# Gated linear attention, then a multiplicative FFN: keeping x in SBUF and starting the FFN's gates earlier

## The chip, the cores and the metric

The kernel runs on one core of a Trainium2 chip. The time is the device time of one execution in microseconds (us), the median of several runs. Engines are named as in the profile: PE is TensorE (PEld its weight load), DVE is VectorE, ACT is ScalarE, POOL is GpSimd, and SP is SyncE, which issues nearly all DMAs here.

## The reference, cut to what matters

```python
B, H, S, D = 4, 8, 768, 48                    # q, k, v, alpha
n_tokens, d_model, d_ff = 3072, 384, 1024     # w1, w2: [384, 1024]; w3: [1024, 1024]; w_out: [1024, 384], in float64

for t in range(S):
    state = alpha[:, :, t, :, None] * state + einsum('bhd,bhe->bhde', k[:, :, t], v[:, :, t])
    y[:, :, t] = einsum('bhd,bhde->bhe', q[:, :, t], state)
x = y.transpose(0, 2, 1, 3).reshape(B * S, H * D)
a = x @ w1
b = x @ w2
h = a * b @ w3
return (h @ w_out).astype(float32)
```

The recurrence is linear in the state. The kernel works it off in chunks of 128 time steps: inside a chunk by scores and a mask, between chunks by a state of 48 x 48 per head. There are 4 x 6 = 24 chunks. Three chunks of x, 384 tokens, form a group; the FFN's gates (x @ w1 times x @ w2) work on one of the 8 groups and 128 of the 1024 columns at a time, so there are 64 gate tiles. w3 is folded into w_out once (8 folds), and the output is 24 blocks of 128 tokens. The weights w1, w2, w3, w_out arrive as float64 and are converted on chip from their bit patterns.

## The kernel before

x of one chunk is left by TensorE in two PSUM banks: bank i holds heads of parity i, with 64 partitions per head (48 of them used), two heads one above the other, and two such pairs (j) along the free dimension. ScalarE copies the banks to SBUF, and two DMAs per chunk write them to DRAM in an order in which the 384 rows are head by head, 48 rows each. A group is loaded back as 3 blocks of 128 rows.

```python
ps = pool("ps", 8, space=PSUM)
xp = pool("xp", 1)
work = pool("work", 2, ...)
xd = [dram.tile([DM, TG], FP32, name=f"xd{g}") for g in range(NG)]        # DM = 384, TG = 384

def to_fp32(dst, *srcs):                       # float64 to float32, in steps
    n, m = len(srcs) * srcs[0].shape[1], srcs[0].shape[1]
    raw = rawp.tile([C, n], I64, tag="raw", name="raw")
    for i, src in enumerate(srcs):
        nc.sync.dma_start(out=raw[:, ds(i * m, m)], in_=src)             # L181
    yield
    # ... ScalarE: rest (L189), power (L194); VectorE: mant (L190), power (L193)
    yield
    # ... VectorE: L196, L197, L199
    yield
    return to

def load_gates(kk, c0, n):                     # 12 of these: 3 blocks of rows x 4 x 256 columns, of w1 and w2
    w = yield from to_fp32(None, *(src[ds(kk * C, C), ds(c0, n)] for src in (moe_w1, moe_w2)))
    # ... ScalarE: high part (L207); VectorE: two low parts (L209, L210)

def attend(n):                                 # the last step of chunk n
    # ... 16 matmuls into the banks y[0], y[1] (L364)
    x = work.tile([C, HP, 2, C], FP32, tag="x", name="x")
    for i in range(2):
        nc.scalar.copy(x[:, :, i], y[i])                                 # L368
    x = x.rearrange("p j i t -> p (j i) t")
    g, c = divmod(n, G)
    to = xd[g].rearrange("(b h d) t -> b d h t", b=2, d=D)
    for half in range(2):
        later.append((to[half, :, :, ds(c * C, C)], x[ds(DP * half, D)]))  # issued by store(), L236

def load_x(g, queue=nc.sync):
    st["xT", g] = xp.tile([C, KM, TG], FP32, tag="xT", name="xT")
    queue.dma_start(out=st["xT", g], in_=xd[g].rearrange("(k p) t -> p k t", p=C))   # L379

def split_x(g, i):                             # x as three float32r parts
    # ... ScalarE 128x1152 (L385), VectorE 128x1152 twice (L386, L387)

def exact(w, x, width, done, keep):            # 6 matmuls, a ScalarE scaling of the bank, 3 more matmuls later
    # ... L402, L403 (ScalarE), L408

def gate(g, f):                                # a gate tile: two pieces
    # first: exact(w1) then ScalarE r (L420);  second: exact(w2) then VectorE ab = bank * r (L424), stored (L436)
```

The main loop runs a chunk per turn and fills TensorE with pieces of gate tiles (`run`) and VectorE and ScalarE with steps of the weight conversion (`convert`). Groups 0 to 3 get half of their 8 tiles here, group 4 all 8, one group every four chunks:

```python
begin = {4 + 4 * g: (g, range(FH if g < 4 else KF)) for g in range(5)}    # FH = 4, KF = 8
for n in range(N + 1):
    store()
    # ... loads of inputs, four chunks ahead
    if n:
        attend_state(n - 1)                     # L358
    if n < N:
        scores(n)                               # L339 (PE), L342 (DVE)
    transposed(n + 1)                           # L299 (PE), L301 (ACT)
    if n - 2 in begin:
        g, tiles = begin[n - 2]
        split_x(g, 0)
        fill.extend(gate(g, f) for f in tiles)
    pieces = (0, 3, 3, 2)[(n - 6) % 4] if n > 5 else 0
    if not pieces:
        settle()
    # ...
    early = n < 7
    convert(1, 2 if n == 0 else 3)
    advance(n)
    if n:
        attend(n - 1)                           # L364
    outer(n)                                    # L311
    run(pieces > 0)
    if early:
        convert(1)
    decayed(n + 2)                              # L277
    logs(n + 4)                                 # L246, L250, L251
    if n in begin:
        load_x(begin[n][0])
    convert(early and n > 2)
    run(pieces > 1)
    decays(n + 3)                               # L261 or L264 (PE), L267, L268 (ACT)
    convert(early or n % 3 == 0)
    run(pieces > 2)
store()
```

Then come the rest of the tiles, with the conversions of w_out and w3 and the folds between them (L456, L462), and at the end the output blocks (L402, L408 again, with other operands, L480 to L482, L490).

```python
visits = [(g, range(FH, KF)) for g in range(4)] + [(g, range(KF)) for g in range(len(begin), NG)]
# ...
    owed += 2.7 if folds or folded else 1.2     # conversion steps per tile
```

Of the kernel before, what the change touches and what calls it, by code (L numbers as in the profile page):

```python
# [10 lines left out]
FP32 = mybir.dt.float32  # L11
# [37 lines left out]
def kernel(  # L49
# [24 lines left out]
    NG = N // G  # L74
    TG = G * C
    CW = 512
# [5 lines left out]
    def pool(name, bufs, stack=ctx, **kw):  # L82
        return stack.enter_context(tc.tile_pool(name=name, bufs=bufs, **kw))


    const = pool("const", 1)
    xp = pool("xp", 1)
    tr = [pool("tr0", 1)]
    gw = pool("gw", 2)
    abp = pool("abp", 3)  # L90
    dram = pool("dram", 1, space=DRAM)
# [7 lines left out]
    work = pool("work", 2, stack=part1, side="right", reuse_waits="tile")  # L99
# [4 lines left out]
    st = {}  # L104
# [2 lines left out]


    ends = {n: dram.tile([3, DM], FP32, name=f"ends{n}") for n in range(2, N, 2) if n % NCH}
    xd = [dram.tile([DM, TG], FP32, name=f"xd{g}") for g in range(NG)]  # L110
    abd = [dram.tile([C, KF, TG], FP32, name=f"abd{g}") for g in range(NG)]

    vs = [p1.tile([C, H, DP], FP32, name=f"v{i}") for i in range(AHEAD + 1)]
# [61 lines left out]

    def to_fp32(dst, *srcs):

        n, m = len(srcs) * srcs[0].shape[1], srcs[0].shape[1]
        raw = rawp.tile([C, n], I64, tag="raw", name="raw")
        for i, src in enumerate(srcs):  # L180
            nc.sync.dma_start(out=raw[:, ds(i * m, m)], in_=src)  # L181
        yield
        words = raw.bitcast(U32).rearrange("p (n w) -> p n w", w=2)
        low, high = words[:, :, 0], words[:, :, 1]

        mant = cvt.tile([C, n], FP32, tag="mant", name="mant")
        top = mant.bitcast(U32)
        rest = cvt.tile([C, n], FP32, tag="rest", name="rest", bufs=2)
        nc.scalar.activation(rest, low, AF.Copy, scale=2.0 ** -52)  # L189
        nc.vector.tensor_scalar(top, high, 0x000FFFFF, 0x00100000, op0=ALU.bitwise_and, op1=ALU.bitwise_or)  # L190
# [12 lines left out]
    def load_gates(kk, c0, n):  # L203
        w = yield from to_fp32(None, *(src[ds(kk * C, C), ds(c0, n)] for src in (moe_w1, moe_w2)))
        w = w.rearrange("p (i n) -> p i n", i=2)
        h, l, m = (w12[:, x, :, kk, ds(c0, n)] for x in range(3))
        nc.scalar.activation(h, w, AF.Copy, scale=(1.0 - 2.0 ** -13) / P)  # L207
        yield
        nc.vector.scalar_tensor_tensor(l, h.bitcast(FP32), -P, w, op0=ALU.mult, op1=ALU.add)  # L209
        nc.vector.scalar_tensor_tensor(m, h.bitcast(FP32), P + 1.0, w, op0=ALU.mult, op1=ALU.subtract)  # L210
# [3 lines left out]
    def convert(steps, ahead=3):  # L214

        for _ in range(steps):
            while weights and len(begun) < ahead:
                begun.append(weights.popleft())
                next(begun[-1])
            if not begun:  # L220
                return
            x = begun.popleft()
            try:
                next(x)
                begun.appendleft(x)
            except StopIteration:
                pass


    later = deque()  # L230

    def store():

        while later:
            dst, src = later.popleft()
            nc.sync.dma_start(out=dst, in_=src)  # L236

    def last(n):
        return n % NCH == NCH - 1
# [105 lines left out]
    HP = NP // 2  # L345
# [15 lines left out]
    def attend(n):  # L361
        (y, heads), ms, vc = st.pop(("y", n)), st.pop(("ms", n)), st.pop(("v", n))
        for j, i, to in heads:
            nc.tensor.matmul(to, vc[:, 2 * j + i, :], ms[:, i, j, :], start=(n % NCH == 0 and j % HP == 0),  # L364
                             stop=(j % HP == HP - 1), skip_group_check=True)
        x = work.tile([C, HP, 2, C], FP32, tag="x", name="x")
        for i in range(2):
            nc.scalar.copy(x[:, :, i], y[i])  # L368
        x = x.rearrange("p j i t -> p (j i) t")

        g, c = divmod(n, G)
        to = xd[g].rearrange("(b h d) t -> b d h t", b=2, d=D)
        for half in range(2):
            later.append((to[half, :, :, ds(c * C, C)], x[ds(DP * half, D)]))


    def load_x(g, queue=nc.sync):
        st["xT", g] = xp.tile([C, KM, TG], FP32, tag="xT", name="xT")
        queue.dma_start(out=st["xT", g], in_=xd[g].rearrange("(k p) t -> p k t", p=C))  # L379

    def split_x(g, i):
        x = st.pop(("xT", g))
# [9 lines left out]
    def settle(keep=0):  # L392

        while len(pending) > keep:
            pending.popleft()()
# [40 lines left out]
            nc.sync.dma_start(out=abd[g][:, f, :], in_=ab)  # L436

    def load_out(j):
        yield from to_fp32(lambda: wo[:, j, :], moe_w_out[ds(j * C, C), :])

    def load_w3(i, c0):
        def to():
            if ("w3", i) not in st:
                st["w3", i] = foldp.tile([C, DF], FP32, tag="w3", name="w3", bufs=2)
            return st["w3", i][:, ds(c0, CW)]
        yield from to_fp32(to, moe_w3[ds(i * C, C), ds(c0, CW)])
        if c0 + CW == DF:
            folds.append(fold(i))

# [76 lines left out]
    load_a(4)  # L526


    begin = {4 + 4 * g: (g, range(FH if g < 4 else KF)) for g in range(5)}

    for n in range(N + 1):
        store()
        load_v(n + AHEAD - 1)
        load_a(n + 5)
        load_kq(n + AHEAD)
        if n:
            attend_state(n - 1)
        if n < N:
            scores(n)
        transposed(n + 1)  # L540
        if n - 2 in begin:
            g, tiles = begin[n - 2]
            split_x(g, 0)
            fill.extend(gate(g, f) for f in tiles)
        pieces = (0, 3, 3, 2)[(n - 6) % 4] if n > 5 else 0
        if not pieces:
            settle()
        if n == 0:
            logs(2)
            decays(2)  # L550
            logs(3)
        early = n < 7
        convert(1, 2 if n == 0 else 3)
        advance(n)
        if n:
            attend(n - 1)
        outer(n)
        run(pieces > 0)
        if early:
            convert(1)  # L560
        decayed(n + 2)
        logs(n + 4)
        if n in begin:
            load_x(begin[n][0])
        convert(early and n > 2)
        run(pieces > 1)
        decays(n + 3)
        convert(early or n % 3 == 0)
        run(pieces > 2)
    store()  # L570
    part1.close()

# [6 lines left out]
    wo = foldp.tile([C, KF, DM], FP32, name="wo")  # L579
    folds, folded = deque(), 0  # L580
    for j in range(KF):
        weights.append(load_out(j))
# [2 lines left out]
            weights.append(load_w3(i, c0))  # L585

    todo, order = list(fill), []
    visits = [(g, range(FH, KF)) for g in range(4)] + [(g, range(KF)) for g in range(len(begin), NG)]
    for k, (g, tiles) in enumerate(visits):
        order.append((max(len(todo) - 3, order[-1][0] + 1 if order else 0), len(todo), g, 1 - k % 2))  # L590
        todo += [gate(g, f) for f in tiles]
    owed = 0.0
    load_x(order[0][2])
    lastp = None
    for i, x in enumerate(todo):
        while order and i >= order[0][0]:
# [57 lines left out]
```

## Time and profile before

| | |
|---|---|
| time, median of 3 | 497.07 us (496.25 to 497.3) |
| span of the profiled execution | 496.3 us |
| mean granted TensorE clock | 0.988 |
| x stores (L236) between 30 and 180 us | 42 DMAs of 96 KB |
| x loads (L379), all | 12 DMAs of 576 KB |
| packets of all DMAs | 160,493, of these 104,640 under 512 B |

A row of the timeline gives the start, the time from the first start to the last end, the engine, the line, what is written and read, and how many instructions were put together. In the table of stretches each engine has its busy time and, in parentheses, its instructions. Matmuls overlap, so the busy time of PE counts an array that is filled loosely as full; the distance from one start to the next says more. A wait is printed as who waited for whom: the sum in us, how often, the longest.

### The profile page before, as it was taken

The page shows a single profiled execution, that of the slowest core. Times are in us where ns is not written, and L with a number is a line of the kernel's source. Part 1 is how long each engine was busy: PE and PEld are TensorE (multiplying, and loading weights), DVE is VectorE, ACT ScalarE, POOL GpSimd, SP SyncE. Part 2 cuts the span into 40 slices and gives each one's busy share as a digit, 9 for nine tenths or more (in the row PEclk, how much of TensorE's full clock was granted, in tenths as well). Part 3 has the DMA queues.
Part 4 walks back from the last instruction along what each step waited for, and adds up shares of the span by engine and source line. Part 5 has one row for each costly group of instructions (what it writes and reads, how often), then busy time and mean ns, then how long its engine had stood idle before and what let it go on. Part 6 is the DMA issues. An engine that isn't in the chain of part 4 may idle for free.

```text
span 496.3 us, 9720 instructions
## 1 busy us (share of the span) xinstructions
PE 465.9 (94%) x3760; PEld 423.1 (85%) x3760; DVE 310.4 (63%) x492; ACT 274.4 (55%) x543; POOL 39.3 (8%) x83
## 2 busy tenths in 40 slices
PE   3778789999999989989999999999999999999997
PEld 1566569898999979979999988888888999999996
DVE  2769899866768447979533455754211756677773
ACT  2666668787777556667755554554333533333330
POOL 2122132121203100000000000000000000000000
PEclk9989799999999999999999999999999999999999
DMA  9999999999999964766533333320002755656521
GB/s 172 186 192 201 234 209 196 234 184 221 194 223 174 218 190 145 226 208 214 184 110 110 111 118 116 116 91 32 33 32 82 227 167 171 178 171 176 177 86 63
DMA packets 160493, 79.08 MB, mean 159 GB/s; under 512 B 104640, under 2 KB 154304, under 8 KB 160448
## 3 DMA queue, kind: packets, MB, share of 16 engines
q1 hardware_dynamic: 159168, 78.40, 63.1%
q0 software_dynamic: 1280, 0.08, 0.5%
q8 instruction: 29, 0.48, 0.4%
q14 instruction: 16, 0.13, 0.1%
HBM read 56.40 MB, written 22.06 MB: 158 GB/s over the span
## 4 chain that ended last, share of the span: by engine, by line
PE 65%; DMA 5%; DVE 2%; issue 1%; ACT 1%; SPq 0%; ACTq 0%
PE bank L402 33%; PE bank L408 16%; PE bank L462 8%; DMA raw<-in_moe_w_dram 4%; PE bank L364 2%; DMA raw<-in_moe_w_out_dram 2%; PE bank L339 2%; PE bank L456 1%; PE bank L358 1%; PE bank L299 1%; DVE power L197 1%; PE bank L311 1%; PE bank L264 0%; DVE mant L196 0%; DVE ab L424 0%
## 5 line engine op out<-in xcount | busy, mean ns | idle before, releaser
L402 PE MATMUL bank<-x,w 128*128 128x384 f32 x768 | 157.8, 341 | 0.0
L402 PEld LDWEIGHTS bank<-x,w 128*128 128x128 f32 x768 | 134.2, 188 | 3.4 <-issue 0.3
L403 ACT ACTIVATE bank<-bank 128x384 f32<-128x384 f32 x152 | 72.0, 475 | 88.8 <-PE bank L402 88.0
L408 PE MATMUL bank<-x,w 128*128 128x384 f32 x384 | 87.9, 339 | 2.5 <-ACT bank L403 2.4
L424 DVE TENSOR_TENSOR ab<-bank,r 128x384 f32<-128x384 f32 x64 | 35.5, 555 | 65.1 <-PE bank L408 33.8
L408 PEld LDWEIGHTS bank<-x,w 128*128 128x128 f32 x384 | 67.4, 188 | 5.5 <-ACT bank L403 4.7
L402 PE MATMUL bank<-w3o,ab 128*128 128x384 f32 x384 | 70.3, 334 | 0.0
L402 PEld LDWEIGHTS bank<-w3o,ab 128*128 128x128 f32 x384 | 66.9, 188 | 0.0
L462 PE MATMUL bank<-wo,w3T 128*128 128x384 f32 x128 | 42.6, 486 | 0.0
L189 ACT ACTIVATE rest<-raw 128x512 f32<-128x512 uint32 (+1 forms) x36 | 23.2, 647 | 33.8 <-DMA raw<-in_moe_w_dram 28.6
L481 DVE TENSOR_TENSOR ab<-abl,ab 128x1024 fp32r<-128x1024 f32 x24 | 29.4, 1225 | 12.3 <-ACT ab L480 12.3
L408 PE MATMUL bank<-w3o,ab 128*128 128x384 f32 x192 | 37.0, 334 | 0.0
L462 PEld LDWEIGHTS bank<-wo,w3T 128*128 128x128 f32 x128 | 24.2, 189 | 14.9
L480 ACT ACTIVATE ab<-abl 128x1024 fp32r<-128x1024 f32 x24 | 25.4, 1060 | 20.3 <-PE bank L408 20.2
L339 PEld LDWEIGHTS bank<-qkT 48*128 48x128 f32 x384 | 25.9, 200 | 9.3 <-ACT qkT L301 4.4
L339 PE MATMUL bank<-qkT 48*128 48x128 f32 x384 | 30.8, 300 | 3.1 <-ACT qkT L301 3.1
L408 PEld LDWEIGHTS bank<-w3o,ab 128*128 128x128 f32 x192 | 33.6, 188 | 0.0
L301 ACT COPY qkT<-bank 128x512 f32<-128x512 f32 x48 | 26.1, 586 | 12.1 <-PE bank L299 12.1
L420 ACT ACTIVATE r<-bank 128x384 f32<-128x384 f32 x64 | 31.2, 488 | 1.7
L342 DVE TENSOR_TENSOR ms<-bank,keep 128x512 int32<-128x512 int32 x48 | 31.0, 683 | 1.7 <-PE bank L339 1.6
L194 ACT ACTIVATE power<-power,rebias 128x512 uint32<-128x512 uint32 (+1 forms) x36 | 24.5, 697 | 12.5 <-DVE power L193 12.2
L277 DVE TENSOR_TENSOR qk<-kq,e 128x768 f32<-128x768 f32 x24 | 22.9, 953 | 11.5 <-ACT e L268 10.5
(69 smaller groups left out, 532.4 us busy)
## 6 DMA issues: line engine op xcount, KB each, us to landing
abd<-ab SPq DMA_DIRECT2D x64, 192.0 KB, 3.4
abl<-abd SPq DMA_DIRECT2D x24, 512.0 KB, 4.5
raw<-in_moe_w_dram SPq DMA_DIRECT2D x16, 512.0 KB, 5.0
xT<-xd SPq DMA_DIRECT2D x12, 576.0 KB, 5.0
raw<-in_moe_w_dram SPq DMA_DIRECT2D x24, 256.0 KB, 4.7
ac<-in_alpha_dram SPq DMA_DIRECT2D x24, 192.0 KB, 5.2
kq<-in_k_dram SPq DMA_DIRECT2D x24, 192.0 KB, 5.4
kq<-in_q_dram SPq DMA_DIRECT2D x24, 192.0 KB, 4.6
```

The lines of the kernel that those rows point to most:

```text
L194: nc.scalar.activation(power, power, AF.Relu, scale=2.0 ** 23, bias=rebias)
L301: nc.scalar.copy(qkT[:, :, :, ds(DP * half, DP)], tp[half])
L339: nc.tensor.matmul(sc[i][:, j, :], qkT[r, 0, j, :], qkT[r, 1, j, :], start=True, stop=True)
L342: nc.vector.tensor_tensor(ms[:, i].bitcast(I32), sc[i].bitcast(I32), keep_bc, op=ALU.bitwise_and)
L402: nc.tensor.matmul(p, w[part][i], x[part][i], start=(part == i == 0), stop=(part == 1 and i == n - 1))
L403: nc.scalar.activation(p, p, AF.Copy, scale=1.0 + 1.0 / P)
L408: nc.tensor.matmul(p, w[2][i], x[2][i], start=False, stop=(i == n - 1), skip_group_check=True)
L420: nc.scalar.activation(r[0], p, AF.Copy, scale=P * P)
L424: nc.vector.tensor_mul(ab, p, r[0])
L462: nc.tensor.matmul(po, w3T[:, j, :], wo[:, j, :], start=(j == 0), stop=(j == KF - 1))
L480: nc.scalar.activation(t[:, 0], ab, AF.Copy, scale=1.0 - 2.0 ** -13)
L481: nc.vector.tensor_sub(t[:, 1], ab, t[:, 0].bitcast(FP32))
```

## The change

x of a group stays in one SBUF tile of three blocks of 128 rows, the layout that the gates read. Each block holds four runs of rows: for each half, 48 rows of one head, which ScalarE copies straight out of PSUM to where they are, and 16 rows of a fourth head. The fourth head of each half (bank 1, second pair) is copied to a tile x4 and moved by six small SBUF to SBUF DMAs per group into the 16 rows that the 48-row heads leave free in each half block. So the rows of x are in another order than before, and the rows of w1 and w2 are loaded in the same order, each block in four runs for each of the two matrices. Groups 0, 1, 2, 4 and 6 are gated within the recurrence straight from SBUF (0 and 1 half of their tiles, the others all 8); those that are needed later (0, 1, 3, 5, 7) are also stored, as they lie, and loaded again after the recurrence. The gates begin at chunk 4, and how many pieces and conversion steps go into each chunk is set by tables. It is meant to take traffic off the DMA queues and to give TensorE gate work earlier.

```diff
-    xp = pool("xp", 1)
+    xp = pool("xp", 2)
-    xd = [dram.tile([DM, TG], FP32, name=f"xd{g}") for g in range(NG)]
+    xd = [dram.tile([C, KM, TG], FP32, name=f"xd{g}") for g in range(NG)]
...
 def to_fp32(dst, *srcs):
         for i, src in enumerate(srcs):
-            nc.sync.dma_start(out=raw[:, ds(i * m, m)], in_=src)
+            for rows, part in src:
+                nc.sync.dma_start(out=raw[rows, ds(i * m, m)], in_=part)
...
     def load_gates(kk, c0, n):
-        w = yield from to_fp32(None, *(src[ds(kk * C, C), ds(c0, n)] for src in (moe_w1, moe_w2)))
+        rows = [(ds(DP * half + to, m), ds(half * DM // 2 + at, m)) for half in range(2)
+                for to, at, m in ((0, D * kk, D), (D, D * KM + (DP - D) * kk, DP - D))]
+        w = yield from to_fp32(None, *([(to, src[at, ds(c0, n)]) for to, at in rows] for src in (moe_w1, moe_w2)))
...
     def store():
-        while later:
+        for _ in range(len(later)):
             dst, src = later.popleft()
             nc.sync.dma_start(out=dst, in_=src)
+        later.extend(stores)
+        stores.clear()
...
     def attend(n):
-        x = work.tile([C, HP, 2, C], FP32, tag="x", name="x")
-        for i in range(2):
-            nc.scalar.copy(x[:, :, i], y[i])
-        x = x.rearrange("p j i t -> p (j i) t")
         g, c = divmod(n, G)
-        to = xd[g].rearrange("(b h d) t -> b d h t", b=2, d=D)
-        for half in range(2):
-            later.append((to[half, :, :, ds(c * C, C)], x[ds(DP * half, D)]))
+        if c == 0:
+            st["xT", g] = xp.tile([C, KM, TG], FP32, tag="xT", name="xT")
+            st["x4", g] = work.tile([C, TG], FP32, tag="x4", name="x4")
+        x, x4, t = st["xT", g], st["x4", g], ds(c * C, C)
+        nc.scalar.copy(x4[:, t], y[1][:, 1])
+        nc.scalar.copy(x[:, 1, t], y[1][:, 0])
+        nc.scalar.copy(x[:, 0:KM:2, t], y[0])
+        if c == G - 1:
+            R = DP - D
+            for half in range(2):
+                for kk in range(KM):
+                    later.append((x[ds(DP * half + D, R), kk, :], x4[ds(DP * half + R * kk, R), :]))
+            if g in kept:
+                stores.append((xd[g], x))
...
-    begin = {4 + 4 * g: (g, range(FH if g < 4 else KF)) for g in range(5)}
+    early = [(0, range(FH)), (1, range(FH)), (2, range(KF)), (4, range(KF)), (6, range(KF))]
+    kept = {0, 1, 3, 5, 7}
+    begin = dict(zip((4, 8, 11, 17, 23), early))
+    pieces = dict(zip(range(4, N + 1), (1, 2, 2, 3, 2, 3, 3, 2, 2, 3, 3, 3, 3, 2, 3, 3, 3, 3, 2, 2, 3)))
+    paces = [3] * 3 + [4] * 4 + [2] * 3 + [3] * 6 + [0] * 9
...
-        if n - 2 in begin:
-            g, tiles = begin[n - 2]
+        if n in begin:
+            settle()
+            g, tiles = begin[n]
             split_x(g, 0)
             fill.extend(gate(g, f) for f in tiles)
-        pieces = (0, 3, 3, 2)[(n - 6) % 4] if n > 5 else 0
-        if not pieces:
-            settle()
+        parts = pieces.get(n, 0)
...
-        convert(1, 2 if n == 0 else 3)
+        pace = paces[n]
+        convert(pace > 0, 2 if n == 0 else 3)
...
-        run(pieces > 0)
-        if early:
-            convert(1)
+        run(parts > 1)
+        convert(pace > 2)
         decayed(n + 2)
         logs(n + 4)
-        if n in begin:
-            load_x(begin[n][0])
-        convert(early and n > 2)
-        run(pieces > 1)
+        convert(pace > 3)
+        run(parts > 2)
         decays(n + 3)
-        convert(early or n % 3 == 0)
-        run(pieces > 2)
+        convert(pace > 1)
+        run(parts > 0)
     store()
+    store()
...
-    visits = [(g, range(FH, KF)) for g in range(4)] + [(g, range(KF)) for g in range(len(begin), NG)]
+    visits = [(0, range(FH, KF)), (1, range(FH, KF)), (3, range(KF)), (5, range(KF)), (7, range(KF))]
...
-        owed += 2.7 if folds or folded else 1.2
+        owed += 3.2 if folds or folded else 1.7
```

More of the change, by code (lines that the diff above doesn't have):

```diff
@@ L176, in to_fp32 @@
     def to_fp32(dst, *srcs):
-        n, m = len(srcs) * srcs[0].shape[1], srcs[0].shape[1]
+        m = srcs[0][0][1].shape[1]
+        n = len(srcs) * m
         raw = rawp.tile([C, n], I64, tag="raw", name="raw")
         for i, src in enumerate(srcs):
-            nc.sync.dma_start(out=raw[:, ds(i * m, m)], in_=src)
+            for rows, part in src:
+                nc.sync.dma_start(out=raw[rows, ds(i * m, m)], in_=part)
         yield
@@ L227, in convert @@
                 pass
-    later = deque()
+    later, stores = deque(), []
     def store():
-        while later:
+        for _ in range(len(later)):
             dst, src = later.popleft()
             nc.sync.dma_start(out=dst, in_=src)
+        later.extend(stores)
+        stores.clear()
     def last(n):
@@ L365, in attend, with load_x @@
                              stop=(j % HP == HP - 1), skip_group_check=True)
-        x = work.tile([C, HP, 2, C], FP32, tag="x", name="x")
-        for i in range(2):
-            nc.scalar.copy(x[:, :, i], y[i])
-        x = x.rearrange("p j i t -> p (j i) t")
         g, c = divmod(n, G)
-        to = xd[g].rearrange("(b h d) t -> b d h t", b=2, d=D)
-        for half in range(2):
-            later.append((to[half, :, :, ds(c * C, C)], x[ds(DP * half, D)]))
-    def load_x(g, queue=nc.sync):
+        if c == 0:
[12 more added lines that the diff above has]
+                stores.append((xd[g], x))
+    def load_x(g):
         st["xT", g] = xp.tile([C, KM, TG], FP32, tag="xT", name="xT")
-        queue.dma_start(out=st["xT", g], in_=xd[g].rearrange("(k p) t -> p k t", p=C))
+        nc.sync.dma_start(out=st["xT", g], in_=xd[g])
     def split_x(g, i):
@@ L438, in load_out @@
     def load_out(j):
-        yield from to_fp32(lambda: wo[:, j, :], moe_w_out[ds(j * C, C), :])
+        yield from to_fp32(lambda: wo[:, j, :], [(slice(None), moe_w_out[ds(j * C, C), :])])
     def load_w3(i, c0):
@@ L445, in to @@
             return st["w3", i][:, ds(c0, CW)]
-        yield from to_fp32(to, moe_w3[ds(i * C, C), ds(c0, CW)])
+        yield from to_fp32(to, [(slice(None), moe_w3[ds(i * C, C), ds(c0, CW)])])
         if c0 + CW == DF:
@@ L551 @@
             logs(3)
-        early = n < 7
-        convert(1, 2 if n == 0 else 3)
+        pace = paces[n]
+        convert(pace > 0, 2 if n == 0 else 3)
         advance(n)
```

## The prediction

> **What bounds the kernel now.** I read the page first (busy shares and the 40 slices), then the table of stretches, then TensorE's timeline in two places, then the waits of the early stretch, then the DMA table.
>
> ```profile
> PE 465.9 (94%) x3760; PEld 423.1 (85%) x3760; DVE 310.4 (63%) x492; ACT 274.4 (55%) x543; POOL 39.3 (8%) x83
> ...
> PE   3778789999999989989999999999999999999997
> ...
> DVE  2769899866768447979533455754211756677773
> ...
> PEclk9989799999999999999999999999999999999999
> DMA  9999999999999964766533333320002755656521
> ```
>
> TensorE is the engine that sets the end. Its slices are below 9 only in the first seventh; there VectorE is at 7 to 9, the granted clock dips, and the DMA engines are full until slice 14 or so (180 us). So I ask how much of the span is not TensorE work at its own best pace. That pace is seen where nothing disturbs it:
>
> ```profile
> 195.30 1.20 PE L402 MATMUL bank<-x,w 128*128 128x384 f32 x6
> 196.34 0.68 PE L408 MATMUL bank<-x,w 128*128 128x384 f32 x3
> 196.86 1.20 PE L402 MATMUL bank<-x,w 128*128 128x384 f32 x6
> ```
>
> From start to start, half a gate tile (a "piece", 9 matmuls) takes 196.86 - 195.30 = 1.56 us. In the same way I read the dense stretches of the timeline: one recurrence chunk is about 4.0 us (L358 0.60, L339 0.99, L299 0.59, L364 0.93, L311 0.55, L264 0.34), one fold of w3 into w_out 5.16 + 0.87 us (chain of waits, L462 and L456), one output chunk 4.16 us. Sum: 128 pieces x 1.56 = 199.7, 24 chunks x 4.0 = 96, 8 folds x 6.03 = 48.2, 24 output chunks x 4.16 = 99.8, together 444 us. The span is 496.3, so 52 us are lost, and the change can only win from these 52.
>
> Where do they lie? The first gate matmul:
>
> ```profile
> 55.08 1.06 PE L299 MATMUL bank<-ident,qk 64*128 64x64 f32 x16
> 56.08 1.97 PE L364 MATMUL bank<-ms,v 128*64 128x128 f32 x16
> ...
> 63.18 1.09 PE L364 MATMUL bank<-ms,v 128*64 128x128 f32 x16
> 64.10 0.62 PE L311 MATMUL bank<-v,qk 128*64 128x48 f32 x16
> 64.65 2.38 PE L402 MATMUL bank<-x,w 128*128 128x384 f32 x12
> ```
>
> Up to 64.65 us TensorE has done 35 us of recurrence work (7 to 10 of each group at the paces above, the ten early L261 pairs at 0.84), so 29.6 us are lost before the first gate: some 16 up to 30 us, while inputs arrive, and some 14 between 30 and 64.65. Note also the same 16 L364 matmuls at 1.97 and at 1.09 us: cold and warm clock. From 64.65 to 200 us there are 121 us of work in 135 us, 14 lost. After 200 us, 8 are lost, 3.6 of them after the last matmul.
>
> What is full between 30 and 65 us, and what between 90 and 150?
>
> ```profile
> 30.00:60.00 30.00, 23.42 (x317) 18.43 (x317) 26.01 (x48) 20.81 (x45) 7.15 (x14) 0.83 1.01 205
> 60.00:90.00 30.00, 26.41 (x320) 23.42 (x320) 26.32 (x44) 23.21 (x51) 8.18 (x11) 1.00 1.09 221
> 90.00:120.00 30.00, 30.00 (x390) 27.46 (x386) 20.37 (x33) 22.93 (x51) 5.38 (x11) 1.00 0.99 210
> 120.00:150.00 30.00, 29.17 (x373) 26.19 (x373) 23.30 (x40) 22.44 (x50) 4.40 (x7) 1.00 0.95 203
> ```
>
> The columns are PE, PEld, DVE, ACT, POOL, the granted clock and the DMA share. Early it is VectorE (26.0 of 30 us, converting the weights) and the DMA engines; from 90 us on TensorE itself. DMA is at 1.0 throughout, but that alone doesn't make it the bound: inputs are fetched four chunks ahead, and the waits of 12 to 60 us name it only for
>
> ```profile
> ACT rest L189 <- DMA raw<-in_moe_w_dram: 5.0, 3, 2.8
> DVE mant L190 <- DMA raw<-in_moe_w_dram: 4.8, 2, 4.2
> ```
>
> and for GpSimd's small round trips.
>
> **What the Trainium skill says.** "DMA: Bandwidth & Descriptors", section Specifications, wants at least 512 B per transfer for line rate. The trace agrees: inputs come in rows of 192 B, and between 30 and 180 us the hardware queue's packets took 96.5% of the engines' time for 208 GB/s, while from 390 to 420 us long rows give 200 GB/s at a share of 0.69. The same page, "Why a DMA increments its semaphore by 16 and not by 1", spreads a DMA over the largest number up to 16 that divides its rows; so I expect pieces of 48 and 16 rows still to use all engines. No run here shows it yet. "TensorE: Matmul & The Clock Gate", Part 1, says that the idle array falls to half clock; the 1.97 against 1.09 us above agrees, and the clock of 0.83 from 30 to 60 us.
>
> **The change part by part.**
>
> *Gates begin sooner.* Before, group 0 is split at chunk 6 and its pieces run from chunk 7 on; 38 pieces run inside the recurrence. After, it is split at chunk 4, with 1, 2, 2 pieces at chunks 4, 5, 6, and 53 in all. The 15 more pieces (23 us) only win where they fill a hole; elsewhere they lengthen the recurrence by what they save later. The holes are those of chunks 4 to 6, some 43 to 64 us: 5 pieces x 1.56 = 7.8 us. Against it stands VectorE, which is full there: the split (L386 and L387, 1.36 + 1.35) and two L424 (1.1) add 3.8 us in a stretch where the weight conversions keep the old pace. Part of this only comes earlier. I count 7.8 - 3.8 = 4 us, and 1.5 more for a warm clock (L339, L299, L364 each lost about 1 us per cold chunk, some two chunks).
>
> *x stays in SBUF.* Between 30 and 180 us the 42 stores of x are 42 x 192 = 8064 packets and the 5 loads 1920, of 94,774: 10.5%. Groups 2, 4, 6 never go to DRAM; the five others are stored in long rows and loaded once or twice less. Two x splits of 12 fall away (1.17 on ScalarE and 2.7 on VectorE each), off the bound. Since DMA rarely ends a wait, I give the relief 2 us: the waits for raw weights (9.8 us summed on two engines, partly overlapping) shorten by a fifth.
>
> *Conversions.* Chunks 7 to 15 take 2 to 3 steps instead of 1 to 2, none after. VectorE then needs about 8.0 us per chunk from 10 to 15 (L342 1.28, L277 0.95, L251 0.55, L321 0.35, L424 0.7, split 0.9, three quarters of a 4.3 us conversion 3.2) and TensorE 4.0 + 2.67 x 1.56 = 8.2. Both are full, so some jitter is felt: I charge 1 us.
>
> *Costs.* The permuted rows turn each of 12 pairs of loads into 8 DMAs: 72 more issues of about 0.33 us (fastest L181), 24 us of SP's queue, which already shows 33 us of issuing in 32 from 30 to 62 us, though most of that is back pressure. The stores that vanish (0.88 per chunk) pay for about half. The inputs behind the first two conversions come 1 us later; I charge 1. Before the split at chunk 4 ScalarE must wait for the six moves, queued when the last copy of x is done and landing perhaps 4.3 us later (median of the x stores): 0.5 us felt. One more ScalarE copy per chunk, about 0.12 us, lies beside other work.
>
> *After the recurrence* fewer tiles remain (37.5 for 45), conversions run at 1.7 and 3.2 steps per tile for 1.2 and 2.7. VectorE needs 1.7/3 x 2.9 + 0.56 = 2.2 us per 3.1 us tile, so it stays hidden. I give 2 us back here: the DMA waits around 206 to 234 us cost TensorE some 3 us, and a queue without x traffic before them should shed most.
>
> Sum: -4 - 1.5 - 2 + 1 + 1 + 0.5 - 2 = -7 us, 490.0 us.
>
> **The rivals.** *TensorE was full already*: the 15 pieces only move. For it: 30.00 of 30 busy from 90 us. Then only chunks 4 to 6 count and costs eat them: 494 to 497. *SP's queue becomes the bound*: 24 us of extra issues in the first 16 chunks delay inputs. For it: SP is busy all of 30 to 62 us. Against: a DMA of 512 KB takes 0.33 us to issue when nothing holds it. It would give 500 to 508. *DMA was the true bound of the recurrence*: 10.5% of 150 us comes free, and the holes (some 32 us of the 52, without the first 16 and the last 3.6) close by a third to a half: 478 to 484. For it: a share near 1.0. Against: the waits hardly name it, and TensorE is full from 90 us.
>
> **Range and chances.** I weigh my sum most, TensorE full next, DMA bound next, SP last. 80% range 482 to 498. Faster by 2% needs under 487.1; chances 0.26 faster, 0.70 within, 0.04 slower.
>
> **What would show it.** The first gate matmul near 50 us instead of 64.65, clock 0.9 or more from 30 to 60 us, DMA share in the recurrence down by a tenth, the last recurrence matmuls (L364 at 192.61 us before) some 18 us later (23 us of pieces less 5 us of filled holes), and the rest shorter by 25. If that last L364 comes hardly later, DMA was the bound and I am too slow; if the first gate is not before 58 us, or the first scores start later by over 2 us, SP or the moves cost more than I charged.

## The result and the profile after

The changed kernel takes 517.01 us (median of 4 runs, 516.71 to 517.91), the kernel before 497.19 us on the same chip (496.25 to 499.98). The ratio is 1.039, interval 1.035 to 1.044: slower by 20 us, where 490 us were predicted and 482 to 498 allowed.

The page of the changed kernel first, busy shares and slices of 12.9 us:

```profile
PE 473.4 (92%) x3760; PEld 428.8 (83%) x3760; DVE 308.3 (60%) x488; ACT 273.6 (53%) x565; POOL 36.1 (7%) x83
...
PE   3786089899999999999999999999999999999996
...
DVE  2666846867675454627799456754312647766763
...
PEclk9996559989999999999999999999999999999999
DMA  9978697977877678312967443320004826555521
```

TensorE's fifth slice, 51 to 64 us, is a 0: it does almost nothing there, and the clock is at half or little more in it and its neighbours. The DMA engines, at 9 in the first fourteen slices before, are now between 6 and 9 there. The table of stretches (columns PE, PEld, DVE, ACT, POOL, clock, DMA share, GB/s) says the same:

```profile
30.00:60.00 30.00, 16.08 (x222) 12.74 (x218) 21.71 (x39) 16.69 (x37) 7.03 (x13) 0.72 0.81 152
60.00:90.00 30.00, 22.98 (x227) 19.36 (x229) 18.94 (x30) 14.80 (x32) 3.30 (x7) 0.71 0.81 158
90.00:120.00 30.00, 28.19 (x330) 25.47 (x328) 21.80 (x36) 20.46 (x48) 3.99 (x8) 0.94 0.83 168
120.00:150.00 30.00, 29.65 (x327) 27.14 (x324) 22.66 (x39) 22.29 (x54) 5.52 (x10) 1.00 0.75 155
```

Between 30 and 60 us TensorE (16.1 for 23.4 us), VectorE (21.7 for 26.0), ScalarE (16.7 for 20.8) and the DMA share (0.81 for 1.01) are all below what they were before. When all of them slacken at once, the bound is to be sought outside these columns. TensorE's timeline shows what it waits for (in brackets the idle time before the row and who ended it):

```profile
36.24 0.62 PE L317 MATMUL bank<-v,qk 128*64 128x48 f32 x16
41.67 1.65 PE L267 MATMUL bank<-la,after 128*128 128x384 f32 x2 [4.81 <-ACT la L252]
...
48.93 1.04 PE L317 MATMUL bank<-v,qk 128*64 128x48 f32 x16
52.48 0.92 PE L267 MATMUL bank<-la,utri 128*128 128x384 f32 x2 [2.51 <-ACT la L252]
66.70 1.33 PE L414 MATMUL bank<-x,w 128*128 128x384 f32 x3 [13.30 <-ACT x L397]
```

The waits of TensorE from 12 to 110 us, the two costliest:

```profile
PE bank L414 <- ACT x L397: 15.1, 2, 13.3
PE bank L267 <- ACT la L252: 10.8, 3, 4.8
```

Two kinds of hole. In some chunks TensorE waits for la, the logarithm of alpha (10.8 us; 2.9 before). And at the first gate matmul it stands for 13.3 us for the split of x (L397): TensorE works its instructions in order, so the recurrence work queued behind that matmul stands too. The first gate comes at 66.70 us, later than the 64.65 us of before.

SP's timeline gives the rest. First the kernel before, then the changed one (SP issues the loads of w1 and w2 at L181 and L183, the inputs at L124 to L136, the moves of the fourth heads at L240):

```profile
43.13 0.42 SPq L136 DMA_DIRECT2D v<-in_v_dram  x1
43.60 0.78 SPq L124 DMA_DIRECT2D ac<-in_alpha_dram  x1
44.43 2.86 SPq L130 DMA_DIRECT2D kq<-in_k_dram  x1
47.34 0.65 SPq L131 DMA_DIRECT2D kq<-in_q_dram  x1
48.08 1.15 SPq L181 DMA_DIRECT2D raw<-in_moe_w_dram  x2
49.33 0.88 SPq L236 DMA_DIRECT2D xd<-x  x2
```

```profile
23.68 10.40 SPq L183 DMA_DIRECT2D raw<-in_moe_w_dram  x16
...
36.75 4.66 SPq L183 DMA_DIRECT2D raw<-in_moe_w_dram  x8
41.70 0.50 SPq L136 DMA_DIRECT2D v<-in_v_dram  x1
42.35 0.47 SPq L124 DMA_DIRECT2D ac<-in_alpha_dram  x1
42.91 0.82 SPq L130 DMA_DIRECT2D kq<-in_k_dram  x1
43.78 0.99 SPq L131 DMA_DIRECT2D kq<-in_q_dram  x1
44.87 5.72 SPq L183 DMA_DIRECT2D raw<-in_moe_w_dram  x8
...
54.03 4.20 SPq L183 DMA_DIRECT2D raw<-in_moe_w_dram  x8
58.27 3.77 SPq L240 DMA_DIRECT2D xT<-x  x6
```

Both queues are almost without gaps (at most 0.3 us between the rows shown), but of different stuff. Before, the longest row of a turn is the load of k, 2.1 us on average over three turns. The tile that it writes had long been free (the load at 44.43 us overwrites inputs last read at 27.83 us), and the DMA engines are full (share 1.01), so I take it for back pressure. After, that load takes 0.7 us on average, so little back pressure is left; most of the time is the issuing itself, 0.42 us for a short load (median of L183). Between 23.68 and 58.27 us the five conversions' 40 loads take 25.0 us of SP's 34.6, 5.0 us per conversion, for some 1.7 us before (10.3 us for six conversions' 12 loads between 22.76 and 57.68 us). Three turns from one load of v to another take 28.0 us (34.12 to 62.13), 9.3 each, where they took 23.2 (35.85 to 59.03), 7.7 each. The Trainium skill, "Perfetto Trace Analysis", What "DMA-bound" means, lists this as a bound of its own: an issuing engine whose track is solid with DMA slices is busy making descriptors, not moving data. The trace agrees: SP solid, DMA share down from 1.01 to 0.81. But SP was as solid before, so a solid track alone does not tell issuing from back pressure; the DMA share and the length of single issues do.

The whole loss lies within the recurrence. Its last L370 matmuls:

```profile
237.29 1.09 PE L370 MATMUL bank<-ms,v 128*64 128x128 f32 x16
```

They start 45 us later than before (192.61), where 18 were foretold. Of the 27 us too many, some 17 lie before the first gate (66.70 us for near 50), the rest after it. From there to the end are 277.6 us for 303.7: 26 shorter, as foretold.

### The profile page after: what moved, and what is told of

It is laid out like the page before. It is cut to its first block, busy times and chain, and to the rows that moved or that the text cites. A ratio compares the mean times of both kernels' runs of the same rounds, so it can differ in the third digit from the quotient of the medians.

```text
span 514.9 us, 9876 instructions
## 1 busy us (share of the span) xinstructions
PE 473.4 (92%) x3760; PEld 428.8 (83%) x3760; DVE 308.3 (60%) x488; ACT 273.6 (53%) x565; POOL 36.1 (7%) x83
## 4 chain that ended last, share of the span: by engine, by line
PE 72%; DMA 9%; DVE 7%; ACT 6%; SPq 3%; issue 2%; DVEq 0%; ACTq 0%
PE bank L414 34%; PE bank L420 16%; PE bank L474 8%; DMA raw<-in_moe_w_dram 4%; PE bank L345 3%; PE bank L370 3%; DMA raw<-in_moe_w_out_dram 3%; PE bank L305 2%; SPq L183 2%; DMA ac<-in_alpha_dram 2%; PE bank L364 2%; PE bank L317 1%; DVE power L199 1%; PE bank L468 1%; ACT x L397 1%
## 5 line engine op out<-in xcount | busy, mean ns | idle before, releaser
L414 PE MATMUL bank<-x,w 128*128 128x384 f32 x768 | 163.6, 348 | 16.0 <-ACT x L397 16.0
L414 PEld LDWEIGHTS bank<-x,w 128*128 128x128 f32 x768 | 135.8, 191 | 22.3 <-ACT x L397 17.5
L420 PE MATMUL bank<-x,w 128*128 128x384 f32 x384 | 87.2, 337 | 0.2 <-ACT bank L415 0.2
L348 DVE TENSOR_TENSOR ms<-bank,keep 128x512 int32<-128x512 int32 x48 | 31.0, 684 | 13.3 <-PE bank L345 13.1
L191 ACT ACTIVATE rest<-raw 128x512 f32<-128x512 uint32 (+1 forms) x36 | 23.3, 647 | 27.5 <-DMA raw<-in_moe_w_dram 20.8
L474 PEld LDWEIGHTS bank<-wo,w3T 128*128 128x128 f32 x128 | 24.2, 189 | 14.9
L494 DVE SCALAR_TENSOR_TENSOR ab<-ab,abl 128x1024 fp32r<-128x1024 f32 x24 | 29.2, 1218 | 0.0
```

What stands on the lines that cost most here:

```text
L348: nc.vector.tensor_tensor(ms[:, i].bitcast(I32), sc[i].bitcast(I32), keep_bc, op=ALU.bitwise_and)
L414: nc.tensor.matmul(p, w[part][i], x[part][i], start=(part == i == 0), stop=(part == 1 and i == n - 1))
L420: nc.tensor.matmul(p, w[2][i], x[2][i], start=False, stop=(i == n - 1), skip_group_check=True)
L474: nc.tensor.matmul(po, w3T[:, j, :], wo[:, j, :], start=(j == 0), stop=(j == KF - 1))
L494: nc.vector.scalar_tensor_tensor(t[:, 2], t[:, 0].bitcast(FP32), -1.0 - 1.0 / P, ab, op0=ALU.mult, op1=ALU.add)
```

## The experiments

The theory to test (S): the 72 extra issues on SP's queue make each chunk's inputs late, and the moves, behind them in the same queue, make the first gate late. Rivals: the moves alone (M); the tables, which ask too much too early (T). In the diffs only the core is shown; the times of before beside the runs are 497.0 to 497.4 us throughout.

**Whole rows.** The permuted loads are undone, the rest stays. The gates then multiply rows of x by rows of w1 and w2 in another order; the work is the same.

```diff
-        rows = [(ds(DP * half + to, m), ds(half * DM // 2 + at, m)) for half in range(2)
-                for to, at, m in ((0, D * kk, D), (D, D * KM + (DP - D) * kk, DP - D))]
+        rows = [(slice(None), ds(kk * C, C))]
```

> The changed kernel with w1 and w2 loaded in plain order, 128 rows in one DMA, 2 DMAs for a conversion in place of 8. Leaves out the permutation of the rows, so the gates multiply the wrong rows; work and schedule are the same. Theory S (SP's queue: 72 more issues at 0.46 us each are 33 us of a serial queue that bounds the first 100 us): 486 to 494 us, the first gate matmul near 52 us in place of 66.7. Theory M (the moves: TensorE waits in order for a split whose x has to be moved first): stays above 508. Theory T (the tables of pieces and steps fill chunks that were full): stays at 513 to 517.

503.03 us, ratio 1.012 (1.010 to 1.014). T falls, M falls; S has the direction and not the size. The same bytes in as many rows of the same length, by a quarter of the DMAs, give 14 us back, and 6 stay. What stays is at the first gate, first in TensorE's timeline, then in SP's:

```profile
54.85 1.33 PE L413 MATMUL bank<-x,w 128*128 128x384 f32 x3 [10.44 <-ACT x L396]
```

```profile
44.82 2.55 SPq L183 DMA_DIRECT2D raw<-in_moe_w_dram  x2
47.47 3.77 SPq L239 DMA_DIRECT2D xT<-x  x6
```

TensorE stands for 10.4 us. The six moves take 3.8 us to issue and are out at 51.2 us only.

**The kernel before with its loads cut in eight.** Each load of 128 rows becomes 48 + 16 + 48 + 16; x still goes through DRAM.

```diff
+            cuts = (0, 48, 64, 112, 128) if len(srcs) == 2 else (0, 128)
+            for p, e in zip(cuts, cuts[1:]):
+                nc.sync.dma_start(out=raw[p:e, ds(i * m, m)], in_=src[p:e])
```

> The kernel before with only its loads of w1 and w2 cut into runs of 48, 16, 48, 16 rows in plain order: 96 DMAs in place of 24, same bytes, same packets, same result. Theory S: slower by 15 to 30 us, 512 to 527, and SP's queue solid up to some 100 us. Theories M and T: 497 to 500, since neither moves nor tables are in it.

554.9 us is the median, but three of the four executions were slow ones near 555 us, so I go by the fourth, 546.1 us. That is 49 us for 72 issues, 1.6 to 3.3 times what S said. Here SP also has the stores of x in its queue, and in the trace (an execution of 555.12 us) it stands at them until x is there, 22.1 us in three places between 12 and 130 us, with the next chunk's inputs behind.

**No moves.** The changed kernel without the 48 moves; the fourth heads' rows of x stay zero.

```diff
-                    later.append((x[ds(DP * half + D, R), kk, :], x4[ds(DP * half + R * kk, R), :]))
+                    pass
```

> The changed kernel without the 48 moves of the fourth heads, whose rows stay zero; all else as it is, 8 loads for a conversion. Theory S: the moves are 6 issues of 0.6 us for a group, two groups in the crowded stretch, so 508 to 514. Theory M: 490 to 500, the 13 us wait for the split gone. Theory T: 515 to 517.

518.49 us, ratio 1.039 (1.033 to 1.045): nothing is won. S and M both miss; the number is nearest to T, which the whole rows have ruled out. Yet the stand at the first gate is gone. The waits of TensorE from 12 to 110 us:

```profile
PE bank L267 <- ACT la L252: 14.5, 5, 6.0
PE bank L270 <- ACT la L256: 3.6, 1, 3.6
PE bank L414 <- DVE x L398: 1.1, 1, 1.1
```

The wait for the split went from 15.1 us (changed kernel, same view) to 1.1, and those for la from 10.8 to 18.1. I read it so: the inputs come when SP gets to them, and a hole closed earlier only opens later.

**Short runs issued by ScalarE.** The 16-row loads go to ScalarE's queue.

```diff
+                queue = nc.scalar if part.shape[0] == DP - D else nc.sync
+                queue.dma_start(out=raw[rows, ds(i * m, m)], in_=part)
```

> The changed kernel with the 16-row runs of w1 and w2 (half of the 96 loads) issued from ScalarE's queue, the 48-row runs from SP as they are. Same DMAs, same result. Theory S: 48 of the issues leave SP, 22 us of its queue; part comes back as ScalarE time, 497 to 507. Theories M and T: 513 to 520.

515.38 us, ratio 1.032 (1.025 to 1.039), far from S. ScalarE's own timeline shows why:

```profile
27.21 3.18 ACTq L184 DMA_DIRECT2D raw<-in_moe_w_dram  x4
31.11 2.20 ACTq L184 DMA_DIRECT2D raw<-in_moe_w_dram  x4
...
38.67 2.92 ACTq L184 DMA_DIRECT2D raw<-in_moe_w_dram  x2
```

```profile
30.43 0.59 ACT L308 COPY qkT<-bank 128x512 f32<-128x512 f32 x1 [2.72 <-DMA raw<-in_moe_w_dram]
...
41.65 0.49 ACT L275 ACTIVATE e<-bank 128x384 f32<-128x384 f32 x1 [2.82 <-DMA kq<-in_q_dram]
```

Two to four issues hold ScalarE's queue for 2 to 3 us, and its own work behind them, here the copy of qkT and the exponential e, stands that long; the stand at the first gate is 15.4 us.

**Whole rows and no moves.** Both burdens taken away, with what each of the two runs above leaves out.

> The changed kernel with plain loads of w1 and w2 (2 DMAs for a conversion) and without the moves of the fourth heads: leaves out the permutation and the fourth heads' rows of x. What is left of the change are the tables and x in SBUF. Theory Q (with plain loads, what remains lost is the 10.4 us for which TensorE's queue stands at the first gate, whose x waits for moves that stand in SP's queue behind loads): 492 to 497. Theory T (the tables themselves cost): 501 to 504, as with the moves.

492.79 us, ratio 0.992 (0.989 to 0.995): faster than before by 0.8%. With the first three this makes a square:

| | no moves | moves |
|---|---|---|
| whole rows, 2 loads per conversion | 492.79 | 503.03 |
| runs, 8 loads per conversion | 518.49 | 517.01 |

The loads alone cost 25.7 us, the moves alone 10.2, both together 24.2 (by the ratios to before 23.5, 9.9 and 23.5). They aren't a sum: with 8 loads per conversion, so I read the waits above, the stand at the first gate lies where TensorE would wait for inputs anyway. In this run the gates begin as they were meant to, and the clock holds:

```profile
44.18 0.97 PE L413 MATMUL bank<-x,w 128*128 128x384 f32 x3
```

```profile
30.00:60.00 30.00, 24.88 (x339) 20.70 (x340) 27.68 (x49) 23.71 (x56) 6.57 (x13) 0.94 1.07 212
```

**Whole rows, begun one chunk later.** Moves kept; group 0 begins at chunk 5.

```diff
-    begin = dict(zip((4, 8, 11, 17, 23), early))
+    begin = dict(zip((5, 8, 11, 17, 23), early))
```

> Plain loads again (rows of w not permuted, so the gates multiply wrong rows), moves kept, and the first group begun at chunk 5 in place of 4, its 8 pieces at 2, 3, 3. Theory Q: the moves have a chunk's time to land, no stop at the first gate, 493 to 498. If the late issue of the moves is not what stops TensorE: 501 to 504, the stop of 10 us shifted by a chunk.

499.56 us, ratio 1.005 (1.003 to 1.007), between the two expectations: a third of the moves' cost is back, and TensorE still stands 7.7 us.

**x in the reference's row order.** So that whole rows of w1 and w2 are the right ones, ScalarE copies one head per half to its place and the six others are moved, 8 DMAs per group; begun at chunk 5.

```diff
-                    later.append((x[ds(DP * half + D, R), kk, :], x4[ds(DP * half + R * kk, R), :]))
+                        row = first = (NP * half + 2 * j + i) * D
+                        while row < first + D:
+                            kk, p = divmod(row, C)
+                            m = min(first + D - row, C - p)
+                            later.append((x[ds(p, m), kk, :], src[ds(DP * half + row - first, m), :]))
+                            row += m
```

> A whole kernel with the reference's result: x stays in SBUF in the order of the reference's rows, so w1 and w2 are loaded in plain order, 2 DMAs for a conversion; two heads are copied in place, the other six moved by 8 SBUF transfers for a group in place of 6; gates begin at chunk 5. Theories S and Q together: 493 to 499. If moves are as costly as loads in short runs: over 503.

503.16 us, ratio 1.013 (1.009 to 1.018): 14 us better than the changed kernel with the whole computation done, but over the 493 to 499 expected, and TensorE still stands at the first gate:

```profile
56.95 1.33 PE L424 MATMUL bank<-x,w 128*128 128x384 f32 x3 [8.37 <-ACT x L407]
```

**The kernel before with each load cut in two.** 24 issues more, no other difference.

> The kernel before with each of the two loads of a conversion cut into two runs of 64 rows: 48 DMAs in place of 24, same bytes and result. Theory S as a lead that is lost (SP runs ahead of the chunks until its work per chunk is longer than a chunk; then inputs come late in every chunk): 24 issues more fit in, 497 to 503. Theory S as a plain price per issue (57 us for 72 issues, as the cut into 8 showed): 513 to 519.

516.82 us, ratio 1.043 (1.036 to 1.050). The plain price holds here, the threshold falls: 19.8 us for 24 issues, 0.8 us each. The signature is that of the changed kernel: L263, which waits for la, stands 10.0 us in five places (2.9 us in three before), and the clock from 30 to 60 us is 0.68.

**Alpha one chunk earlier.** Alpha has the shortest lead of all inputs. In the changed kernel it is now asked for one chunk sooner.

```diff
-        load_a(n + 5)
+        load_a(n + 6)
```

> The changed kernel with each chunk's alpha asked for one chunk earlier (six ahead instead of five); nothing else moves, and no DMA is added or removed. Theory L (the short loads cost through lead: alpha has the shortest lead of all inputs, one chunk, so it is what arrives late, and TensorE's waits for la follow): 507 to 511 us, and the 10.8 us of L267 waiting for la between 12 and 110 us mostly gone. Rival R (SP simply cannot issue everything of the first 100 us in the time, so an earlier alpha only makes k, q or the weights later): 514 to 519 us, another wait takes the place of the one on la.

519.32 us, ratio 1.046 (1.040 to 1.051). Alpha's lead was not it; the result fits a rate. The waits of TensorE from 12 to 110 us:

```profile
PE bank L414 <- ACT x L397: 18.6, 2, 16.8
PE bank L305 <- DVE qk L283: 7.6, 1, 7.6
PE bank L267 <- ACT la L252: 3.5, 1, 3.5
```

The waits for la fell from 10.8 to 3.5 us as ordered, and k and q (qk) and the split took their place. That is what R says: SP has a fixed amount to issue, and what is put forward puts something else back.

**Short runs issued by GpSimd**, the engine that is busy 7% of the span, and then **the moves as well**. Both compute all of it.

```diff
+                queue = nc.gpsimd if part.shape[0] == DP - D else nc.sync
+                queue.dma_start(out=raw[rows, ds(i * m, m)], in_=part)
```

> The changed kernel with the 16-row runs of w1 and w2 (48 of the 96 loads) issued from GpSimd's queue instead of SP's; GpSimd is busy 7% of the span. Same transfers, same rows, same bytes. Theory R (time on SP's queue is what the loads cost): about half or two thirds of the 14 us of the loads come back, 505 to 510 us. Rival D (the price is in the DMA engines or in the landing, wherever it is issued): 514 to 519 us. If GpSimd's own issuing delays its round trips for the state, more than 519.

> As the run with the 16-row runs on GpSimd's queue, and the 48 moves of the fourth heads go there too, so SP issues only 24 loads more than in the kernel before. Theory R: with both burdens mostly off SP, 495 to 502 us, the wait at the first gate under 4 us. Rival D: 510 us or more. If the moves now stand behind loads in GpSimd's queue as they did in SP's, the wait at the first gate stays over 8 us and the time is 503 to 510.

509.68 us, ratio 1.025 (1.019 to 1.031), and 503.20 us, ratio 1.013 (1.008 to 1.019). The transfers are the same; only who issues them differs, and 7.3 and 13.8 us of the 19.8 come back. So at least the part that comes back doesn't lie in the DMA engines. In the first run TensorE still stands 13.5 us at the first gate. The second is a little over what R expected. There the stand is down from 13.3 to 3.2 us:

```profile
39.73 1.65 PE L271 MATMUL bank<-la,after 128*128 128x384 f32 x2 [6.02 <-ACT la L256]
...
53.57 1.33 PE L418 MATMUL bank<-x,w 128*128 128x384 f32 x3 [3.21 <-ACT x L401]
```

A wait of 6 us for la is still there, with 24 loads more on SP than before. The Trainium skill, "DMA: Bandwidth & Descriptors", Issuing engines are not separate DMA queues, says that spreading DMAs over engines saves only the sequencer's time, usually small beside the transfer. Here that time was the bound, and the saving 7.3 us with half of the loads moved, 13.8 with the moves too.

**The row-ordered version with its moves on GpSimd's queue.**

```diff
+        while moves:
+            dst, src = moves.popleft()
+            nc.gpsimd.dma_start(out=dst, in_=src)
```

> x in the reference's row order in SBUF, w1 and w2 loaded in whole rows (2 DMAs per conversion), group 0 begun at chunk 5, as the version that gave 503.2 us, with its 64 moves issued from GpSimd's queue. Theory R (the moves cost by standing on SP's queue): 493 to 497 us, the level of the version with no moves, and a little faster than before. Rival (the moves cost by their own latency after the last copy of x, whoever issues them): 500 to 505 us.

503.31 us, ratio 1.013 (1.008 to 1.019), as with SP, where R said 493 to 497. The rival's 500 to 505 fits by the number. GpSimd's timeline, then TensorE's:

```profile
44.24 0.60 POOL L337 TENSOR_TENSOR dec<-dec,dec 128x4 f32<-128x4 f32 x1
44.78 4.02 POOL L239 DMA_DIRECT2D xT<-x  x8
48.81 0.52 POOL L338 TENSOR_TENSOR T<-tmp,dec 128x192 f32<-128x192 f32 x1
```

```profile
49.39 1.13 PE L366 MATMUL bank<-qkT,T 48*64 48x128 f32 x16 [3.99 <-POOL T L338]
```

GpSimd's queue is in order too. Its eight issues (4.02 us) stand ahead of the product that advances the state, and TensorE waits 4.0 us for that. ScalarE's timeline shows a second cost:

```profile
51.61 0.37 ACT L380 COPY x<-bank 128x256 f32<-128x256 f32 x1 [6.75 <-DMA xT<-x]
```

The row-ordered version has only one tile for the heads of odd parity, and the copy of the next chunk into it waits until the moves have landed, 11.1 us in three places. Moves issued from GpSimd land 4.0 us after issue at the median, those from SP 2.2. So the run doesn't say what the moves would cost on a free queue, with a second tile.

**The row-ordered version begun at chunk 6, and the kernel before with the same tables.** The first keeps its moves on SP; groups 0, 1, 2, 4, 6 begin at chunks 6, 9, 12, 18, 24. The second has whole rows and x through DRAM, and takes the same begins, pieces and pace of conversions. Both compute all of it.

```diff
+    begin = dict(zip((6, 9, 12, 18, 24), early))
+    pieces = dict(zip(range(6, N + 1), (2, 3, 3, 3, 3, 2, 3, 3, 3, 3, 3, 3, 3, 3, 3, 3, 2, 2, 3)))
```

> x in the reference's row order in SBUF with 8 moves per group on SP's queue, w1 and w2 loaded whole, and the same tables as the kernel before with the new tables, so group 0 is begun at chunk 6 instead of 5. Theory S (TensorE stood 8.4 us at the first gate because its matmuls were queued before the moves had landed; a chunk later they have landed): 494 to 498 us, and no wait over 3 us at the first gate. Rival (the moves delay the inputs and weights behind them on SP's queue all the same): 501 to 505 us.

> The kernel before with the changed kernel's tables (which groups are gated inside the recurrence, 48 pieces there instead of 38, the pace of conversions), each group begun one chunk later since x still goes through DRAM; loads of w1 and w2 whole, no moves. The version of the changed kernel with plain loads and no moves gained 4.3 us. Theory T (the gain came from the tables): 492 to 495 us. Rival X (it came from x staying in SBUF and the earlier first gate): 496 to 500 us.

496.02 us, ratio 0.999 (0.996 to 1.003), and 495.01 us, ratio 0.997 (0.995 to 0.999). For the first, S is right. SP's timeline and TensorE's:

```profile
46.59 6.07 SPq L239 DMA_DIRECT2D xT<-x  x8
52.76 0.53 SPq L136 DMA_DIRECT2D v<-in_v_dram  x1
```

```profile
56.56 2.72 PE L424 MATMUL bank<-x,w 128*128 128x384 f32 x6 [1.64 <-ACT x L407]
```

Eight moves still take 6.07 us of SP's queue, yet TensorE stands 1.6 us at the first gate instead of 8.4, and 7 us of time are gone (later groups begin a chunk later too). So with whole rows the moves' time on the queue costs little; most of what they cost is the matmul queued before they have landed. For the second, the tables alone are worth 2.2 us, at the edge of what T expected; that is half of the 4.2 us of the version without moves. x in SBUF with its moves (496.02) gains nothing over x through DRAM (495.01), though that one still stands 4.3 us at its first gate.

## Why the prediction was wrong

The step that failed is the first under *Costs*: "72 more issues of about 0.33 us …, 24 us of SP's queue …, though most of that is back pressure", charged with 1 us.

- *The duration.* 0.33 us was the fastest load seen. The short loads took 0.42 us at the median and 0.62 on average between 23.68 and 58.27 us (25.0 us for 40).
- *"Most of that is back pressure."* True of before, and the wrong conclusion. The queue of before had no gaps. (The "33 us of issuing in 32" counts two loads of k in full that reach out of the stretch; within it there are some 30.) Back pressure there meant that SP was just keeping up with full DMA engines, not that it had time to spare. When 3.3 us per conversion were added, the loads of k shrank by 1.4 us a turn (6.40 us in three, then 2.23) and the turn still grew from 7.7 to 9.3 us.
- *"The inputs behind the first two conversions come 1 us later; I charge 1."* A once-only delay was assumed. It is a rate: the turns of the first hundred microseconds are longer, as the three measured above. The runs put the term at 14 us with the moves in place and 25.7 without; asking for alpha earlier, which would cure a delay of alpha, cured nothing.
- *The stores.* The stores that were to "pay for about half" do vanish, 0.88 us per turn or 2.6 in three, but every three turns there are six moves, 3.77 us.

That runs of 48 and 16 rows still use all DMA engines, as I expected, no run shows. They land 3.2 and 2.9 us after issue, the whole loads of before after 4.7, so their landing isn't what costs.

*The moves*, charged with 0.5 us for ScalarE's wait: the wait itself was named, its size was not. Moves that stand in one queue behind loads, and a matmul that stands in order before other work, made 13.3 us of it, 10.4 with whole rows. It costs 10.2 us in time with 2 loads per conversion, and with 8 nothing more, since, as I read it, the holes overlap. Begun at chunk 6, even eight moves per group leave the time about 1 us above that of the version that goes through DRAM.

*The gains* had the right direction and about half of the size. Without the two costs the first gate came at 44.18 us (foretold near 50), the clock was 0.94 (0.9 or more), the last L369 of the recurrence at 213.36 us (near 211), and the time 4.2 us below before, where the terms for gates, clock, x in SBUF, conversions and the rest sum to 8.5. Of the 4.2 the tables give 2.2 even with x through DRAM. Where the other 2 come from, x in SBUF or the begin at chunk 4, wasn't separated; without moves nothing allows that begin. The DMA share fell by more than the tenth foretold in the changed kernel, but there because SP fed the engines less; without the two costs it is 1.07, 0.97 and 0.99 from 30 to 120 us (1.01, 1.09 and 0.99 before), and a fifth lower only from 120 us on. The tail was right: 26 us shorter for 25.

*The rivals.* "SP's queue becomes the bound" was right, with 500 to 508 us and the least weight. "Against: a DMA of 512 KB takes 0.33 us to issue when nothing holds it" was no argument against: what counts is how many issues a turn has, not how many bytes. The sign at the end, a first gate not before 58 us, pointed to SP and the moves, and did so here. The other two rivals foretold no loss: TensorE wasn't full but starved, and the DMA share fell without a gain.

Left open: why an issue costs 0.8 us of the time in the kernel before (24 more, 19.8 us) and 0.36 in the changed one without moves (72 more, 25.7 us). Counted in SP's time the gap is smaller, by my estimate from the timelines: the halves add 1.2 us per conversion (17.5 us for six, 10.3 before), 14 us over twelve; the runs add 3.3, some 40 over twelve, of which the absent stores of x (0.88 us a chunk) give back 14 over the sixteen chunks with conversions. For the rest there is a candidate in the trace of the halves: SP stands idle at the stores of x until x is copied, 27.0 us in ten places between 12 and 250 us (4.5 in four before), and the next inputs stand behind. No run takes this stand away.

## What to carry to other kernels

Before more DMAs are put on a queue, read that queue's timeline for gaps: a queue without gaps has no room, whether its time is issuing or back pressure, and each added issue then lengthens the turn for all that stands behind it. Cut a load into row runs only where the queue has gaps. Bringing x itself into order by moves, with whole loads, was the cheaper way here: with the gates begun two chunks later it cost nothing against the kernel before (496.02 us), and gained nothing. And an early start of a side task on an in-order engine is worth only as much as its operands are early: begun one chunk too soon, it stops the main task as well.

## What the runs showed of the hardware

- A load of 16 or 48 rows of 2 KB (32 or 96 KB) takes SP 0.42 us to issue at the median, a move of 16 rows within SBUF 0.58 us. Such a move lands 1.9 us after its issue (median of 48), sooner than I had taken from the x stores (4.3).
- Issued from GpSimd, the same moves take 0.49 us each but land 3.3 us after issue (medians of 48). Short loads issued from ScalarE take 0.39 us at the median and up to 1.56. An engine that computes pays for issuing with its own work: eight moves held GpSimd's for 4.02 us, two loads ScalarE's for 2.92.
- A load of 64 rows of 2 KB takes SP 0.60 us to issue (median of 24), more than one of 16 or 48 rows. Cutting 24 loads of 128 rows in two halves, the same bytes and the same rows, made a kernel of 497 us 4% slower.
